# A fused windowed attention and squared-ReLU MLP on one NeuronCore: the written-out order of all engines, banks, buffers and first loads is replaced by another one

## The chip, the core and the metric

The kernel runs on one NeuronCore of a Trainium2 chip. The core has TensorE (PE in the profile, with its weight loads as PEld), VectorE (DVE), ScalarE (ACT), GpSimd (POOL) and SyncE (SP), 16 DMA engines, an on-chip memory of 128 partitions and a small accumulator memory of eight banks. The metric is the device time of one execution in microseconds (us). The profiled execution is described by its span, from the first to the last instruction.

## What is computed

The input is q, k and v of 4 batches, 8 heads, 768 positions and 64 channels. Each position attends to itself and the 95 positions before it, and to the first 8 positions of its batch; a slope per head lowers the scores with distance. The heads are put side by side (3072 tokens of 512 numbers) and go through an MLP with a hidden width of 2048.

```python
scores = scale * np.matmul(q, k.transpose(0, 1, 3, 2))
bias = -slopes[:, None, None] * dist[None, :, :]
scores = np.where(keep, scores + bias[None], -1000000000.0)
a = softmax(scores)                       # over the last axis
x = np.matmul(a, v)                       # heads side by side: [3072, 512]
h = x @ w_in                              # [3072, 2048]
r = np.maximum(h, 0.0)
out = (r * r) @ w_out                     # [3072, 512]
```

## The kernel before

**Attention.** The 3072 tokens are 24 tiles of 128 (tile j, six per batch). For a tile, q and k are brought into transposed form (qkT). For tiles 0 to 7 TensorE does that (words `tr.0.j` for q and `tr.1.j` for k, line 528) and VectorE or ScalarE copies the result out of its bank (`T.n.j`, lines 455 and 453). For tiles 8 to 23 one DMA transpose on SP's queue does it (`T.j`, line 554). Then follow the bias products of tiles 0 to 2 (`bias.j`, line 597), the scores against the tile itself and the one before it (`sc.j`, line 618; those of tiles 7, 13 and 19 ride along with the tile before), four exponentials on ScalarE (`exp.j`, line 684; two for the first tile of a batch), the multiplication with the decay on VectorE (`mul.j`, line 709), the products with v (`pv.j.0`, `pv.j.1`, line 767) and the normalisation on VectorE (`norm.j`, lines 797 and 798). `gk.j` and `gv.j` copy the eight global keys and values of a batch into the tile's own buffers. The finished tile x is transposed again, by TensorE (`trx.j`, line 835, and a copy `xT.j`) for tiles 0 to 7 and by a DMA transpose on SP's queue (`xT.j`, line 859) from tile 8 on.

**MLP.** Two tiles make a block of 256 tokens, 12 blocks. Both layers use a scheme with seven products in the place of eight: sums of operand quarters are made first (`isum` and `wsum` of the weights, `xs` of the inputs, line 939, and `sum` of the hidden values, line 1185, all on VectorE), then seven products (`h.blk.g.p1` to `p7`, line 967, eight matmuls each; `s2.blk.p.g`, line 1230, four matmuls each), which are taken apart again by copies (`u` and `part`, mostly ScalarE), additions (`c`, line 1011, and `o`, line 1305, VectorE), rectifiers (`relu` and `c21`) and squares (`q`, `sq`, mostly ScalarE). Block 0 and half of block 1 use plain products (`s1.blk.s`, line 1081), which need only a slice s of the first weights.

**Loads.** The q and k of tile 0 come over SP's queue (line 343). All else of the first part comes over POOL's queue, one transfer after the other, by line 330 (`ld.q.j`, `ld.k.j`, `ld.v.j`, then `ld.win.s` and `ld.wout.s`, the slices of the two weights; slices 0 and 2 of the first come in two halves). From tile 6 on `load.j` issues v, q and k of a tile (line 334). q and k have three buffers for the tiles from 6 on, so `load.j` waits until tile j-3 has been transposed; v has ten. `gate.j` is a small write of VectorE that stands for a buffer of v being free. Results leave by SP's queue (`st.blk.sub`, line 1327).

**What sets the order.** Nothing is scheduled on the chip. A string of 1230 words, `ORDER`, lists every operation once. The program walks through it and emits each operation to its engine. A word's tail gives the bank (`:3`) or buffer that it takes, and `@A` or `@V` the engine, ScalarE or VectorE, where there is a choice. So the string sets the sequence on each engine's own queue, the banks and buffers, and the engine. The place of a word among words of other engines has no effect. Engines run ahead of each other until a data dependence or a buffer still in use holds them; within an engine the order is strict, so an instruction that waits holds all that stand behind it.

```python
for word in ORDER.split():
    word, _, banks = word.partition(":")
    name, _, letter = word.partition("@")
    o["engine"] = self.ENGINES[letter] if letter else next(iter(o["engines"]))
    o["banks"] = [int(b, 16) for b in banks]
```

Of the kernel before, what the change touches and what calls it, by code (L numbers as in the profile page):

```python
# [57 lines left out]
tr.0.0:0 T.0.0@V tr.1.0:1 bias.0.0:23 T.1.0@V ld.q.1 ld.k.1 tr.0.1:4 T.0.1@V ld.q.2 ld.k.2 E0.1 ld.q.3 ld.v.0 ld.k.3  # L58
tr.1.1:5 T.1.1@A ld.v.1 sc.0.0 bias.1.0:6701 exp.0.1.0:0 sc.1.0 tr.0.2:4 exp.0.0.0 gk.1@A T.0.2@V exp.1.0.0:1 tr.1.2:5
T.1.2@V bias.2.0:3264 sc.2.0 exp.1.1.0 exp.1.1.1:3 ld.k.4 exp.1.0.1 ld.q.4 pv.0.1:5 tr.0.3:7 pv.0.0:1 ld.v.2 gk.2@A  # L60
exp.2.1.1:4 exp.2.0.0:5 exp.2.0.1 exp.2.1.0 tr.1.3:0 T.0.3@V T.1.3@V sc.3.0:4730 norm.0.0:0 norm.0.1 pv.1.0:6 tr.1.4:1
ld.q.5 pv.1.1:2 norm.1.0:1 norm.1.1 trx.0:5 exp.3.1.1:6 ld.k.5 gv.1@A ld.v.3 tr.0.4:0 T.1.4@V T.0.4@V xT.0@A:0 gk.3@V
trx.1:6 exp.3.0.1 exp.3.1.0:7 exp.3.0.0 ld.win.1.0 pv.2.0:2 pv.2.1:5 norm.2.0:0 norm.2.1 gv.2@V mul.3.0:8 sc.4.0:1037
exp.4.1.0:9 trx.2:2 ld.win.4.0 xT.1@A exp.4.1.1:a tr.1.5:4 tr.0.5:5 T.1.5@A exp.4.0.0 xT.2@A:1 mul.3.1:b pv.3.0:0
pv.3.1:6 T.0.5@A s1.0.1:7 norm.3.0:1 gk.4@V exp.4.0.1 norm.3.1 gv.3@A s1.0.1#2 trx.3:4 sc.5.0:0126 exp.5.0.1:c
exp.5.1.0:d s1.0.4:5 exp.5.1.1 E0.0 mul.4.0:e xT.3@V ld.v.4 mul.4.1:f ones.6 pv.4.0:3 s1.1.1:4 relu.0.4@V:2 exp.5.0.0
ld.win.3.0 s1.0.3:2 pv.4.1:1 relu.0.1@A:0 sq.0.1@A:0 gv.4@A s1.0.3#2 mul.5.1:1 s1.1.3:6 norm.4.0:0 norm.4.1 ld.win.2.0
ld.win.0.0 s1.0.0:5 relu.0.3@A:3 sq.0.3@A mul.5.0:5 gate.10 s1.0.2:0 trx.4:7 relu.1.1@A:4 sq.1.1@A:1 xs.1.0:0 ld.v.5
ld.win.2.1 pv.5.0:3 ld.win.0.1 pv.5.1:1 xs.1.1 ld.win.6.0 ld.win.7.0 ld.win.5.0 relu.1.3@A:7 norm.5.0:1 norm.5.1
ld.wout.3 s1.1.2:2 xT.4@A:2 relu.1.2@A:8 ld.wout.2 ld.wout.1 ld.wout.0 isum.0.0 s1.1.0:4 s1.0.2#2 trx.5:3 gate.14  # L70
# [1379 lines left out]
```

## Time and profile before

| what | before |
|---|---|
| runs | 197.19, 198.71 and 276.52 us; the median is 198.71 us |
| span of the profiled execution | 195.7 us; its own run time is not listed, the two lower runs lie 1.5 and 3.0 us above this span |
| matmuls on TensorE | 2808 |
| moved by DMA | 26.92 MB in 111713 packets |
| VectorE, ScalarE, POOL busy | 179.4, 161.6 and 75.1 us |

The third run is far above the other two; the comparison below goes by the lower ones and by the span. The profile has one row for a group of instructions of one engine and line, with its number, busy time and mean duration, and behind a bar the time that the engine idled ahead of them and what ended it. In a timeline row the first number is the start in us from the beginning of the span, the second the length of the row. In the windows view the columns are the stretch, its length, the busy time and instruction count of PE, PEld, DVE, ACT and POOL, the granted clock of TensorE as a share of its full speed, the DMA load and GB/s. Matmuls overlap one another and their ends are modelled, so a busy TensorE need not be one at its peak rate.

### The profile page before, as it was taken

To read this page: it belongs to the slowest core of one execution; us is meant where nothing else is said; L and a number is where in the kernel's file an instruction comes from. 1 tells how busy PE (TensorE), PEld (TensorE's weight loads), DVE (VectorE), ACT (ScalarE), POOL (GpSimd) and SP (SyncE) were. 2 spreads that over 40 slices of the span, in tenths; PEclk is the share of its full clock that TensorE was granted. 3 is DMA by queue.
4 is the path that set the end of the run, shared out by engine and by line. 5 is a ranking of instruction groups with operands and counts; after the bars stand their busy time and mean duration, and the time that the engine had idled before them with its cause. 6 is when DMAs were issued, how large, how long until landed. Compare 5 with 4: busy or idle time off the path is not lost.

```text
span 195.7 us, 6835 instructions
## 1 busy us (share of the span) xinstructions
PE 188.5 (96%) x2808; PEld 170.5 (87%) x2808; DVE 179.4 (92%) x437; ACT 161.6 (83%) x338; POOL 75.1 (38%) x93
## 2 busy tenths in 40 slices
PE   7986999999999999999999999999999999999993
PEld 3774999999888989989989989989889999999982
DVE  8569989999999999989999999899999899999982
ACT  6699999999989797999899997587987798986600
POOL 8999784775564502650047080119200000000000
PEclk9999999999999999999999999999999999999999
DMA  7999999999999999999949989999947440152026
GB/s 125 149 150 167 179 193 205 205 162 151 155 150 143 99 177 168 119 100 227 139 79 129 138 74 119 209 168 97 147 113 188 85 136 13 20 193 105 0 91 234
DMA packets 111713, 26.92 MB, mean 138 GB/s; under 512 B 103234, under 2 KB 108866, under 8 KB 111682
## 3 DMA queue, kind: packets, MB, share of 16 engines
q0 software_dynamic: 80256, 13.37, 91.9%
q1 hardware_dynamic: 31426, 13.11, 33.4%
q8 instruction: 22, 0.36, 0.7%
q14 instruction: 9, 0.07, 0.1%
HBM read 27.26 MB, written 6.29 MB: 171 GB/s over the span
## 4 chain that ended last, share of the span: by engine, by line
PE 85%; POOL 6%; DMA 5%; DVE 1%; issue 0%; POOLq 0%; DVEq 0%
PE bank L1230 37%; PE bank L967 32%; PE bank L1081 6%; PE bank L618 5%; PE bank L767 5%; POOL qk_first L330 5%; DMA win<-in_moe_w_in_dram 3%; DMA xT<-x 2%; POOL v L330 2%; PE bank L835 1%; PE bank L528 0%; DVE xs L939 0%; DVE buf L886 0%; DVE hsum L1185 0%; DVE early L1305 0%
## 5 line engine op out<-in xcount | busy, mean ns | idle before, releaser
L684 ACT ACTIVATE buf<-bank 128x512 bf16<-128x512 f32 x76 | 41.5, 613 | 2.8 <-PE bank L618 2.7
L1031 ACT ACTIVATE hs<-buf 128x512 bf16<-128x512 f32 x62 | 37.2, 635 | 2.5 <-DVE buf L1011 2.0
L1230 PEld LDWEIGHTS <-hsum 128*128 128x128 bf16 x384 | 35.3, 98 | 4.0
L453 ACT COPY buf<-bank 128x512 f32<-128x512 f32 (+1 forms) x59 | 32.1, 569 | 7.7 <-PE bank L967 6.1
L1230 PE MATMUL bank<-wsum,hsum 128*128 128x256 bf16 x288 | 38.0, 273 | 0.0
L1011 DVE CUSTOM_DVE_ANT_0 buf<-bank,buf 128x512 f32<-128x512 f32 x49 | 33.0, 682 | 0.8 <-ACT buf L453 0.3
L967 PEld LDWEIGHTS <-qk_first 128*128 128x128 bf16 x504 | 31.1, 98 | 1.4 <-issue 0.3
L967 PEld LDWEIGHTS <-win 128*128 128x128 bf16 x504 | 30.8, 98 | 0.9
L334 POOL DMA_DIRECT2D qk<-in_q_dram x18 | 16.0, 889 | 35.3 <-DMA qkT<-qk 30.0
L1230 PEld LDWEIGHTS <-hs 128*128 128x128 bf16 x288 | 26.3, 98 | 2.7
L1230 PE MATMUL bank<-wout,hs 128*128 128x256 bf16 x192 | 27.3, 273 | 0.0
L334 POOL DMA_DIRECT2D v<-in_v_dram x18 | 16.0, 891 | 23.1 <-PE bank L967 13.1
L967 PE MATMUL bank<-xs,qk_first 128*128 128x128 bf16 x336 | 24.6, 219 | 0.2 <-DVE buf L886 0.2
L967 PE MATMUL bank<-xT,win 128*128 128x128 bf16 x336 | 24.6, 219 | 0.0
L709 DVE TENSOR_TENSOR buf<-buf,E 128x1024 bf16<-128x1024 bf16 x32 | 21.5, 683 | 0.5 <-ACT buf L684 0.5
L798 DVE TENSOR_TENSOR x<-bank,rs 128x256 bf16<-128x256 f32 x48 | 20.4, 425 | 1.7
L767 PE MATMUL bank<-v,buf 128*128 128x65 bf16 x312 | 16.1, 193 | 0.9 <-DMA v<-in_v_dram 0.5
L1185 DVE TENSOR_TENSOR hsum<-hs 128x1024 bf16<-128x1024 bf16 (+1 forms) x26 | 16.4, 642 | 0.3
L334 POOL DMA_DIRECT2D qk<-in_k_dram x18 | 16.1, 897 | 0.6 <-DMA wout<-in_moe_w_out_dram 0.4
L767 PEld LDWEIGHTS <-buf 128*128 128x128 bf16 x312 | 13.9, 98 | 1.8 <-DVE buf L709 0.6
L884 ACT ACTIVATE buf<-bank 128x512 f32<-128x512 f32 x23 | 13.7, 607 | 1.0 <-PE bank L967 1.0
L453 ACT COPY part<-bank 128x256 f32<-128x256 f32 x29 | 11.1, 383 | 3.6 <-PE bank L1230 3.6
(92 smaller groups left out, 349.4 us busy)
## 6 DMA issues: line engine op xcount, KB each, us to landing
out_dram<-buf SPq DMA_DIRECT2D x17, 256.0 KB, 2.7
v<-in_v_dram POOLq DMA_DIRECT2D x24, 128.0 KB, 5.4
qk<-in_q_dram POOLq DMA_DIRECT2D x18, 128.0 KB, 5.0
qk<-in_k_dram POOLq DMA_DIRECT2D x18, 128.0 KB, 5.5
wout<-in_moe_w_out_dram POOLq DMA_DIRECT2D x8, 256.0 KB, 9.7
win<-in_moe_w_in_dram POOLq DMA_DIRECT2D x6, 256.0 KB, 7.1
out_dram<-early SPq DMA_DIRECT2D x5, 256.0 KB, 2.7
qk_first<-in_q_dram POOLq DMA_DIRECT2D x5, 128.0 KB, 4.6
```

Of the source, the lines that this page charges most:

```text
L334: nc.gpsimd.dma_start(out=dst, in_=src)
L453: nc.scalar.copy(dst, src)
L684: nc.scalar.activation(out=tiles[tag, j, g][:, odd], in_=tiles.pop(("sc", j, odd, g)).rearrange("p a c -> p (a c)"), func=Act.Exp, scale=s ...
L709: nc.vector.tensor_mul(at, tiles.pop(("esc", j, g)), bias)
L767: nc.tensor.matmul(out=po[:, hi, :], lhsT=tiles["at", j, g][:, odd, at * P : (at + 1) * P], rhs=v_sb[kj][:, h, :], start=(i == 0), stop=(i ...
L798: nc.vector.tensor_tensor(out=x[:, 4 * hf : 4 * hf + 4, :], in0=po[:, :, :D], in1=rs.to_broadcast([P, 4, D]), op=Alu.mult,)
L884: nc.scalar.activation(dst, src, Act.Relu)
L967: nc.tensor.matmul(out=tiles["h", blk, g, bank][:, n], lhsT=left_[:, s, k], rhs=right_[:, k], start=opens and n == 0 and k == 0, stop=k == ...
L1011: nc.vector._custom_dve(TENSOR_ADD_SAT, out=hr, in0=src, in1=tiles.pop(("u", blk, g, i)), s0=float("inf"), s1=0.0,)
L1031: nc.scalar.activation(hs, hr, Act.Square)
L1185: nc.vector.tensor_tensor(out=t[:, i, h], in0=t[:, a, h] if isinstance(a, int) else half_a(blk, *a)[:, h], in1=t[:, b, h] if isinstance(b, ...
L1230: nc.tensor.matmul(out=tiles["acc", blk, bank][:, cols], lhsT=left_[:, s], rhs=right_[:, cols], start=first and s == 0, stop=s == NSTEP - ...
```

## The change

Only the string `ORDER` is replaced; not a line of code differs. The 1230 names are the same, so every load, matmul, copy and store is still made once. What differs is the sequence on each engine, the bank and buffer numbers, the order of the first loads and, for some words, the engine. Of the words with a choice of engine VectorE has 11 fewer than before among `c21`, `gv`, `part`, `u`, `sq` and `o.p4`, and 7 more among `T`, `gk`, `xT` and `q`; ScalarE has the balance of four more. The diff holds 111 lines on each side; the first of each side, and the lines that hold the words `T.11` and `xT.9`, read:

```diff
-tr.0.0:0 T.0.0@V tr.1.0:1 bias.0.0:23 T.1.0@V ld.q.1 ld.k.1 tr.0.1:4 T.0.1@V ld.q.2 ld.k.2 E0.1 ld.q.3 ld.v.0 ld.k.3
+ld.k.1 ld.q.1 ld.q.2 ld.k.2 tr.0.0:0 ld.v.0 tr.1.0:1 T.0.0@V ld.k.3 bias.0.0:23 T.1.0@V tr.1.1:0 bias.1.0:4567 ld.v.1
...
-h.3.1.p4 c.3.1.c21@A:1 q.3.1.c11@A c.3.1.c12:6 s2.2.p5.0 pv.9.0:5 gk.9@V T.11 st.0.0 norm.9.0:1 q.3.1.c12@A
-xT.9 norm.10.0:0 xs.4.0:1 xs.4.1 h.4.1.p2:5 pv.10.1:4 q.3.1.c21@A q.3.0.c21@A part.3.p6@A:1 u.4.1.1@A:6 u.4.0.1@A:5
+o.2.p5:9 xT.9 q.3.0.c12@V h.3.0.p4 exp.10.1.0:b s2.3.p1.0:6 exp.10.1.1:e sum.3.2:1 s2.3.p1.1 T.11 o.2.p4@A sum.3.0
```

POOL's queue, ahead of and at the first slices of the first weights (`win`). The names are the load targets; in both versions the rows further up are the other loads of q and k (of tiles 1 to 5, `qk_first`) and v. Before:

```order
L330 DMA qk_first_66<-in_q_dram 128x8x64
L330 DMA v_2_73<-in_v_dram 128x8x64
L330 DMA qk_first_66<-in_q_dram 128x8x64
L330 DMA qk_first_66<-in_k_dram 128x8x64
L330 DMA v_3_74<-in_v_dram 128x8x64
L330 DMA win_93<-in_moe_w_in_dram 128x4x256 x2
L330 DMA v_4_75<-in_v_dram 128x8x64
```

Now:

```order
L330 DMA v_2_73<-in_v_dram 128x8x64
L330 DMA qk_first_66<-in_q_dram 128x8x64
L330 DMA qk_first_66<-in_k_dram 128x8x64
L330 DMA qk_first_66<-in_q_dram 128x8x64
L330 DMA v_3_74<-in_v_dram 128x8x64
L330 DMA win_93<-in_moe_w_in_dram 128x4x256 x2
L330 DMA v_4_75<-in_v_dram 128x8x64
```

In both, five loads of q, five of k and four of v stand ahead of the first `win`. What moved is which of them come first: k of tile 1 now leads, the last q stands one load later and the last k one load earlier, and v of tile 5, just below these rows, now stands behind three slices of the weight instead of behind five pieces of it.

TensorE's queue around the first plain product of the MLP (L1081), with the weight loads. `win_93` is the first weight, `v_3` and `buf_8` belong to the second half of tile 3's product with v, `qkT_5` and `qkT_4` to the scores of tile 5. Before:

```order
L767 LDWEIGHTS buf_8_135
L767 MATMUL bank_6_113<-v_3_74,buf_8_135 128x65
L767 LDWEIGHTS buf_8_135
L767 MATMUL bank_6_113<-v_2_73,buf_8_135 128x65
L1081 LDWEIGHTS win_93
L1081 MATMUL bank_7_114<-xT_0_117,win_93 128x128
```

Now:

```order
L618 LDWEIGHTS qkT_4_85
L618 MATMUL bank_7_114<-qkT_5_86,qkT_4_85 128x128
L618 LDWEIGHTS qkT_4_85
L618 MATMUL bank_4_111<-qkT_5_86,qkT_4_85 128x128
L1081 LDWEIGHTS win_93
L1081 MATMUL bank_1_108<-xT_0_117,win_93 128x128
```

The scores of tile 5, which stood after the first product of the MLP and the transposes of tile 3, now stand directly ahead of it.

SP's queue around block 8. `xT_1` (before) and `xT_0` (now) is the transposed input of block 8 (tiles 16 and 17, from `x_0` and `x_1`), `qkT_8`, `qkT_7` and `qkT_6` are q and k of tiles 20, 19 and 18. Before:

```order
L859 DMA_TRANSPOSE xT_1_118<-x_0_115 128x4x128
L1327 DMA out_0_dram<-buf_11_138 128x512
L554 DMA_TRANSPOSE qkT_8_89<-qk_8_69 128x8x128
L859 DMA_TRANSPOSE xT_1_118<-x_1_116 128x4x128
L1327 DMA out_0_dram<-early_103 128x512
L554 DMA_TRANSPOSE qkT_7_88<-qk_7_68 128x8x128
L1327 DMA out_0_dram<-buf_9_136 128x512
L554 DMA_TRANSPOSE qkT_6_87<-qk_6_67 128x8x128
```

Now:

```order
L859 DMA_TRANSPOSE xT_0_117<-x_0_115 128x4x128
L859 DMA_TRANSPOSE xT_0_117<-x_1_116 128x4x128
L554 DMA_TRANSPOSE qkT_8_89<-qk_8_69 128x8x128
L554 DMA_TRANSPOSE qkT_7_88<-qk_7_68 128x8x128
L554 DMA_TRANSPOSE qkT_6_87<-qk_6_67 128x8x128
L554 DMA_TRANSPOSE qkT_9_90<-qk_6_67 128x8x128
```

The second transpose of block 8's input (tile 17) stood behind a store and the transpose of tile 20; now it stands ahead of tile 20, and no store stands between them. The same kind of exchange is made the other way round further up: the transpose of tile 11 (`T.11`) stood ahead of `xT.9` and now stands behind it, and that of tile 15 now stands behind `xT.12`, where it stood ahead of it.

More of the change, by code (lines that the diff above doesn't have):

```diff
@@ L63 @@
[L63 to L67, printed above, removed]
```

212 lines of the change are left out of this document (109 added, 103 removed).

## The prediction

> **What bounds the kernel now.** I read the totals of the page first, then the windows, then the chain of work that ended last, then the waits of TensorE.
>
> ```profile
> span 195.7 us, 6835 instructions
> PE 188.5 (96%) x2808; PEld 170.5 (87%) x2808; DVE 179.4 (92%) x437; ACT 161.6 (83%) x338; POOL 75.1 (38%) x93
> ```
>
> TensorE is busy for 96% of the span, VectorE for 92%. An average does not say where the missing 7.2 us of TensorE are, so I cut the span at 4.58 us (end of the warm-up matmuls), 19.66 us (first plain product of the MLP) and 192.40 us (end of the last matmul).
>
> ```profile
> 4.58:19.66 15.08, 12.57 (x213) 10.04 (x212) 11.19 (x34) 13.03 (x31) 15.08 (x19) 1.00 2.17 155
> 19.66:192.40 172.74, 172.55 (x2588) 159.23 (x2588) 164.11 (x384) 145.82 (x304) 56.22 (x67) 1.00 1.21 136
> ```
>
> The reader is to see two stages with different limits. In the first, TensorE idles 15.08 - 12.57 = 2.5 us. In the second it idles 0.2 us in 172.7, at a granted clock of 1.00. POOL, which issues the loads, is busy all through the first stage.
>
> ```profile
> 13.60 6.01 DMA win<-in_moe_w_in_dram
> 19.66 1.07 PE bank L1081 x16
> ...
> 35.40 3.13 PE bank L967 x56
> ...
> 123.03 4.44 DMA xT<-x
> 128.31 0.60 DVE hsum L1185
> 128.91 0.61 DVE buf L886
> ...
> 182.77 9.64 PE bank L1230 x88
> ```
>
> The chain says the same. Up to 19.66 us it runs through POOL's issues and the landing of the first weight slice, then through TensorE nearly without a break: a product of 128 columns takes 3.13/56 = 0.056 us and one of 256 columns 9.64/88 = 0.110 us, back to back. One detour is left, at 123 to 129.5 us: the second transpose of block 8's input lands 4.44 us after its issue.
>
> A new order does not shorten a matmul. In the second stage it can win the 0.2 us of shown idle time and what the modelled ends of matmuls hide, some tenths; in the first at most the 2.5 us. After the last matmul both strings have the same words up to the last store. So the most that the change can bring is about 2.7 us of 195.7, or 1.4%, below the 2% that a measurement of this kernel can tell from no change. What it can lose has no such bound.
>
> **The first stage.** The first weight slice is what ends it.
>
> ```profile
> PE bank L1081 <- DMA win<-in_moe_w_in_dram: 0.3, 1, 0.3
> 13.60 1.62 POOL L330 DMA_DIRECT2D win<-in_moe_w_in_dram  x2
> DMA to landing us min/median/max: 6.6/6.6/6.6
> ```
>
> TensorE waited 0.3 us for it. POOL issues it behind 14 loads in the old order and behind 14 in the new one, each of the same size, so it lands at 13.60 + 6.01 = 19.6 us again. The second slice is issued right behind it (the third row is its landing; 14.34 + 6.6 = 20.96 us).
>
> ```profile
> 16.35 0.23 PE L618 MATMUL bank<-qkT 64*128 64x128 bf16 x2
> 20.88 0.23 PE L618 MATMUL bank<-qkT 64*128 64x128 bf16 x2
> 21.44 1.05 PE L1081 MATMUL bank<-xT,win 128*128 128x256 bf16 x8
> ```
>
> These are the starts of tile 4's scores, of tile 5's scores and of the second slice's product. Ahead of that product the same work stands in both orders: all of tiles 0 to 3, the scores of tiles 4 and 5, the first slice's product, the transposes of tiles 0 to 3. So its start compares the two stages. Before, it is 21.44 us.
>
> In the new order tile 4's scores stand behind the transpose of k of tile 5, which is now the 12th load of POOL; the 12th of before was issued at 11.00 us.
>
> ```profile
> 11.00 0.98 POOL L330 DMA_DIRECT2D qk_first<-in_q_dram  x1
> DMA to landing us min/median/max: 5.6/5.6/5.6
> ```
>
> It lands at 16.6 us, and with the transpose and the copy (the row below shows such a copy, 0.6 us on ScalarE) tile 4's scores start near 16.9 us instead of 16.35. Its exponentials are then later by the same half microsecond. Against that, tile 5's scores no longer wait for ScalarE.
>
> ```profile
> 17.58 0.61 PE L528 MATMUL bank<-ident,qk_first 128*128 128x128 bf16 x8
> 18.23 0.60 ACT L453 COPY qkT<-bank 128x512 bf16<-128x512 bf16 x1
> 19.66 0.65 ACT L453 COPY qkT<-bank 128x512 bf16<-128x512 bf16 x1
> L684 ACT ACTIVATE buf<-bank 128x512 bf16<-128x512 f32 x76 | 41.5, 613 | 2.8 <-PE bank L618 2.7
> ```
>
> Before, both transposes of tile 5 were done at 18.2 us, but the second copy ended only at 20.3 us, behind other work of ScalarE. Now both copies are on VectorE. The scores of tile 5 then wait for two exponentials of tile 4 whose banks they take, 41.5/76 = 0.55 us each (last row), which start at 18.5 us behind two copies and a global one of ScalarE, and end near 20.0 us; the first slice's product follows (20.0 to 20.9), the transposes of tile 3 (to 21.1), and the second slice has landed. Its product starts at 21.1 us: **0.3 us gained**. Bounds: it cannot start ahead of the landing at 20.96, so at most 0.45 gained; if the exponentials of tile 4 stay late by the half microsecond to the end, 0.5 lost. I take 0.3, which is what the rows give when followed one by one; the cover is VectorE, which in this stage is busy 11.2 of 15.1 us.
>
> What stands behind (slices 3, 2, 0, then 6, 7, 5 and all of `wout`) lands in the same slots as before. The new order uses several of them within 0.2 us of their landing, so a gain beyond 0.3 us would be taken back there.
>
> **The detour at 123 us.** VectorE waited for the transpose of tile 17's x:
>
> ```profile
> 127.55 0.42 DVE L939 TENSOR_TENSOR xs<-xT 128x512 bf16<-128x512 bf16 x1 [0.52 <-DMA xT<-x]
> 120.48 2.07 SPq L554 DMA_TRANSPOSE qkT<-qk  x1
> 123.03 1.19 SPq L859 DMA_TRANSPOSE xT<-x  x1
> DMA to landing us min/median/max: 2.4/2.7/5.5
> ```
>
> The last row is over all 16 transposes of x. This one took 4.4 us with the transpose of tile 20 ahead of it in flight; the median is 2.7. Now tile 20 comes behind it. It lands 1.7 us sooner; the first consumer of it (`xs.8.0`) stands three products of 0.445 us earlier in TensorE's order, 1.3 us. So the 0.5 us wait goes, and TensorE, which waits for VectorE right behind it (the two DVE pieces of the chain), has most of it: **0.4 us gained**. Bounds: 0.5 gained, or nothing if it is as slow as before. What is late next is VectorE itself, which has no room there.
>
> **Engines exchanged.** VectorE gives four words net to ScalarE, one of 0.3 to 0.7 us each, some 2 us of 179.4. TensorE waits for VectorE only 0.2 us in the second stage, so this is worth 0 to 0.2 us; I take 0. ScalarE, at 83%, covers it.
>
> **Transposes that come later in SP's queue.** This is what the change may cost. T.11 now stands behind xT.9, T.15 behind xT.12, and the scores of tile 17 stand 2.0 us earlier in TensorE's order while T.17 is held by the same load.
>
> ```profile
> 71.39 1.20 SPq L859 DMA_TRANSPOSE xT<-x  x1
> 78.13 0.23 PE L618 MATMUL bank<-qkT 64*128 64x128 bf16 x2
> 96.20 3.03 SPq L859 DMA_TRANSPOSE xT<-x  x2
> 101.04 0.23 PE L618 MATMUL bank<-qkT 64*128 64x128 bf16 x2
> 107.33 1.23 SPq L554 DMA_TRANSPOSE qkT<-qk  x1
> 115.06 0.23 PE L618 MATMUL bank<-qkT 64*128 64x128 bf16 x2
> DMA to landing us min/median/max: 3.1/5.2/6.7
> ```
>
> The last row is over the transposes of q and k; the L618 rows are the scores of tiles 11, 15 and 17. T.11 is issued behind xT.9 at 71.4 + 1.3 = 72.7 us and lands between 75.8 and 79.4 us, 77.9 at the median; the scores are wanted at 78.1 - 0.3 = 77.8 us. xT.12 was issued at 96.2 us, right behind its normalisation; that now stands about 1.8 us earlier, so T.15 goes at 94.4 + 1.2 = 95.6 us and lands between 98.7 and 102.3, against 100.7 us wanted. T.17 goes at 107.3 us and lands between 110.4 and 114.0, 112.5 at the median; it is wanted at 115.06 - 2.0 - 0.3 = 112.8 us. At the medians these waits cost 0.1 to 0.2 us together; at the maxima 1.6 + 1.6 + 1.2 = 4.4 us; at the minima nothing. Behind a waiting score matmul stands all of TensorE's queue. I take **0.2 us lost** and keep both ends.
>
> **The sum.** 195.7 - 0.3 - 0.4 + 0.2 = 195.2 us of span. The two lower runs of before lie 1.5 and 3.0 us above the span of the profiled one; the listed median, 198.7, is the upper of them. With the middle, 2.3, the changed kernel comes to **197.5 us**.
>
> **Rivals.** *Nothing gained:* VectorE is busy 164.1 of 172.7 us, so what TensorE gains in front is waited for behind VectorE, and T.11 eats the rest. Span 195.5 to 196.5, time about 198.2 us. For it: VectorE stands at 95% in the second stage. Against it: it loses 2 us of work.
>
> *Late transposes (slower):* the transposes of q and k meet other traffic and take 6.7 us, not 5.2. The row above has 3.1 to 6.7 us for the same transfer, so it can happen. Then 4.4 us are lost at tiles 11, 15 and 17, and if those of x take 5.5 us in the place of 2.7, the inputs of blocks 6 and 8 are late by some 1.4 us each: 195.7 - 0.3 + 4.4 + 2.8 = 202.6 of span, up to 205 us of time, and some 200 us with half of it. It decides where the landings rise above 5.1 to 5.5 us, the leads of these three tiles. There is a second turn of the screw: a tile's buffer of q and k is filled anew only when its transpose has landed.
>
> ```profile
> POOL qk L334 <- DMA qkT<-qk: 30.0, 6, 9.9
> ```
>
> POOL waited 30 us for that, in six waits, so each late transpose delays a later load as well. Against this rival: T.12 and T.13 have 10 us of TensorE work between their place and their scores, counted from the new order. The Trainium skill, DMA: Bandwidth & Descriptors, section SWDGE vs HWDGE vs iDMA, says that POOL's and SP's transfers feed different queues inside each DMA engine and that the engine takes them in turn. By that rule a transpose that meets a load takes twice the quiet time; the trace agrees, with 3.1 us at the least and 6.7 at the most, but cannot say which of the new places meet one; if all did, the time would be that of this rival.
>
> *All idle time of the front goes:* tiles 0 to 5 pass without a wait and the 2.5 us are won, 192.7 of span, 195 us. Against it stands the first slice at 19.6 us, whose place in POOL's queue is the same. This is also the case in which the change would not do what it seems: the loads are put in another order, but the one that ends the stage stays where it was.
>
> **How the numbers follow.** The forecast (span 194.6 to 195.5) has 0.53, nothing gained 0.26, late transposes 0.18, the front emptied 0.03. The range reaches down to 194.6 + 1.5 = 196.1, and a little below it for half of the last case, 195.6; up to 202.4, which takes in the lower half of the late transposes. Slower by over 2% is above 202.7 us: 0.13. Faster by over 2% is below 194.7 us: 0.03. The rest, 0.84, is within 2%.
>
> **What would show it.** Right: the second slice's product (L1081, 128x256) starts at 21.0 to 21.2 us; the `xs` row near 127 us has no wait for `xT`; TensorE's waits show none above 0.3 us for `qkT` after 20 us. Wrong: a wait of L618 for DMA `qkT<-qk` near 78, 101 or 113 us, a wait of more than 1 us for `win` or `wout` between 20 and 45 us, or a stage after 20 us in which TensorE's busy time falls below 9.8 of 10 us without a DMA named, which would put VectorE's order in the place of the transposes.

## The result and the profile after

The changed kernel takes 198.94 us at the median of 14 runs (198.02 to 200.55), the kernel before 197.51 us at the median of 14. The ratio is 1.0072 with a 95% interval of 1.0047 to 1.0097: slower by 0.7%, which is less than 2% and more than the measurement is uncertain. The ratios, here and below, leave out the slow runs (here one of 276.52 us), and so can differ a little from the ratio of the medians. 197.5 us and a gain of 0.5 us of span had been forecast. The profiled execution of the changed kernel took 198.99 us, so it is a typical one.

First the totals of the page of the changed kernel, then the same two stretches as before (stretch, length, busy time and count of PE, PEld, DVE, ACT and POOL, granted clock, DMA load, GB/s).

```profile
span 197.2 us, 6882 instructions
PE 187.9 (95%) x2808; PEld 170.0 (86%) x2808; DVE 176.9 (90%) x433; ACT 165.8 (84%) x342; POOL 75.1 (38%) x93
```

```profile
4.58:19.66 15.08, 11.68 (x217) 9.63 (x217) 12.70 (x41) 12.56 (x28) 15.08 (x19) 1.00 2.19 158
19.66:193.90 174.24, 172.88 (x2588) 158.91 (x2584) 160.15 (x372) 150.49 (x310) 56.23 (x67) 1.00 1.20 136
```

The span is 1.5 us longer, the same 2808 matmuls run at the same clock of 1.00, and VectorE has 2.5 us less to do. TensorE now idles 3.4 us in the first stretch, where it idled 2.5, and 1.4 us in the second, where it idled 0.2. So the loss is waiting. How it falls on the two stages this cut does not tell, because the first plain product of the MLP now starts at 20.33 us and not at 19.66; the sums further down do. Who was waited for, in waits of TensorE (total us, times, longest), before:

```profile
PE bank L618 <- DVE qkT L455: 0.6, 1, 0.6
...
PE bank L767 <- DMA v<-in_v_dram: 0.5, 1, 0.5
...
PE bank L967 <- DVE buf L886: 0.2, 1, 0.2
```

Now, and in the chain of work that ended last (start, length):

```profile
PE bank L618 <- DVE qkT L455: 1.3, 2, 0.7
PE bank L767 <- DMA v<-in_v_dram: 1.3, 2, 0.9
...
PE bank L967 <- DMA win<-in_moe_w_in_dram: 0.6, 1, 0.6
...
PE bank L967 <- DMA xT<-x: 0.3, 1, 0.3
```

```profile
24.02 8.90 DMA win<-in_moe_w_in_dram
32.99 1.43 DVE qk_first L907 x3
117.87 6.86 DMA xT<-x
```

The first two rows of waits belong to the first stage; the L618 row is longer because tile 4's scores now wait for VectorE's copies. The third row is new: slice 5 of the first weights, the last to be loaded, lands at 24.02 + 8.90 = 32.9 us and first TensorE, then VectorE's sums of the weights wait for it. The same load in the kernel before:

```profile
L330 POOL DMA_DIRECT2D win<-in_moe_w_in_dram x1: 740/740/740, 23.4 to 23.4; - x1
DMA to landing us min/median/max: 7.6/7.6/7.6
```

It landed at 31.0 us, 1.9 us earlier. The last row of the chain is the transposed x of tile 16, which takes 6.9 us. The two places at which the prediction looked:

```profile
21.60 0.28 PE L1081 MATMUL bank<-xT,win 128*128 128x256 bf16 x1
```

```profile
128.07 0.42 DVE L939 TENSOR_TENSOR xs<-xT 128x512 bf16<-128x512 bf16 x1
```

The second slice's product starts at 21.60 us, not at 21.0 to 21.2. VectorE's wait for the transposed x of tile 17 is gone, as forecast (no bracket behind the row), but nothing was won by it.

One trace is one execution. To add up where TensorE loses time I took, for every matmul of a trace, the time from the start of the one before to its own, less the time that such a matmul takes when they run back to back (0.0556 us for 128 columns, 0.109 for 256, and so on), and summed the rest. The first column of sums ends at the second slice's product, ahead of which the same work stands in both orders; some 0.12 us at each change to score matmuls are in all of them. The traces marked 2 and 3 are from the experiments below.

```
us lost by TensorE    start of    up to  from there          53 to  108 to  after
beyond its own rate   2nd slice   it     to 53 us   108 us   130 us  130 us  sum
before                21.44       4.67   0.40       2.17     0.62    1.24    9.11
before, 2             21.30       4.54   0.40       1.84     0.61    1.24    8.64
changed               21.60       4.81   1.53       2.07     0.89    1.27    10.56
changed, 2            20.96       4.13   1.33       1.99     1.34    1.37    10.16
changed, 3            20.81       4.17   0.27       2.21     1.12    1.30    9.07
mean of changed less
mean of before        -0.25       -0.24  +0.64      +0.08    +0.50   +0.07   +1.05
```

On the mean of these traces the first stage wins its quarter of a microsecond. Behind it 0.6 us are lost up to 53 us and 0.5 us between 108 and 130 us. The traces differ by a microsecond among themselves, so the means are rough, and more traces change the first two of them.

Some experiments below alter nothing ahead of 53 us. With them there are six traces of the new order and four of the old for that part (two more of the old are left out, in which the granted clock was 0.66 between 19 and 24 us).

- The second slice's product starts at 20.6 to 22.5 us in the new order and at 21.3 to 21.4 us in the old, at 21.3 us on the mean in both. In the new order it follows the landing of its slice by 0.05 to 0.27 us, in the old by 0.5 to 0.95 us.
- From there to 53 us the loss is 0.2 to 1.5 us in the new order and 0.4 to 0.8 us in the old, some 0.3 us more on the mean.

So neither the gain in front nor the size of the loss up to 53 us is settled. The 0.5 us between 108 and 130 us holds: three more traces of the old order, unaltered there, lose 0.3 to 0.6 us.

### The profile page after: what moved, and what is told of

Its sections match the earlier page's. It is cut to its first block, busy times and chain, and to the rows that moved or that the text cites. A ratio compares the mean times of both kernels' runs of the same rounds, so it can differ in the third digit from the quotient of the medians.

```text
span 197.2 us, 6882 instructions
## 1 busy us (share of the span) xinstructions
PE 187.9 (95%) x2808; PEld 170.0 (86%) x2808; DVE 176.9 (90%) x433; ACT 165.8 (84%) x342; POOL 75.1 (38%) x93
## 4 chain that ended last, share of the span: by engine, by line
PE 76%; DMA 12%; POOL 8%; DVE 2%; issue 1%; DVEq 0%; POOLq 0%
PE bank L1230 36%; PE bank L967 30%; DMA win<-in_moe_w_in_dram 8%; PE bank L618 5%; POOL qk_first L330 5%; PE bank L767 4%; DMA xT<-x 3%; POOL v L330 2%; POOL win L330 1%; DVE qk_first L907 1%; PE bank L528 0%; PE bank L1081 0%; DVE x L798 0%; DVE buf L1305 0%; DVE buf L1011 0%
## 5 line engine op out<-in xcount | busy, mean ns | idle before, releaser
L1031 ACT ACTIVATE hs<-buf 128x512 bf16<-128x512 f32 x54 | 33.1, 638 | 0.9 <-DVE buf L1011 0.5
L453 ACT COPY buf<-bank 128x512 f32<-128x512 f32 (+1 forms) x51 | 28.2, 569 | 6.2 <-PE bank L967 5.2
L684 ACT ACTIVATE buf<-bank 128x512 bf16<-128x512 f32 x54 | 30.3, 615 | 2.0 <-DVE buf L709 1.4
L967 PEld LDWEIGHTS <-qk_first 128*128 128x128 bf16 x504 | 30.5, 98 | 0.7
L334 POOL DMA_DIRECT2D qk<-in_q_dram x18 | 16.0, 888 | 33.8 <-DMA qkT<-qk 30.8
L1230 PE MATMUL bank<-wout,hs 128*128 128x256 bf16 x192 | 25.9, 273 | 0.0
L334 POOL DMA_DIRECT2D v<-in_v_dram x18 | 16.1, 895 | 21.3 <-PE bank L967 12.0
L1011 DVE CUSTOM_DVE_ANT_0 buf<-bank,buf 128x512 f32<-128x512 f32 x32 | 21.4, 684 | 0.4 <-ACT hs L1031 0.2
L684 ACT ACTIVATE early<-bank 128x512 bf16<-128x512 f32 x34 | 19.2, 607 | 1.5 <-PE bank L618 0.9
L884 ACT ACTIVATE buf<-bank 128x512 f32<-128x512 f32 x26 | 15.3, 599 | 3.2 <-PE bank L967 2.0
L453 ACT COPY part<-bank 128x256 f32<-128x256 f32 x32 | 12.2, 382 | 4.1 <-PE bank L1230 4.1
L1305 DVE TENSOR_TENSOR buf<-bank,part 128x256 f32<-128x256 f32 x30 | 12.5, 419 | 1.7 <-PE bank L1230 1.1
L767 PE MATMUL bank<-v,buf 128*128 128x65 bf16 x256 | 12.7, 194 | 1.3 <-DMA v<-in_v_dram 1.3
```

The costliest lines, as they stand in the source:

```text
L334: nc.gpsimd.dma_start(out=dst, in_=src)
L453: nc.scalar.copy(dst, src)
L684: nc.scalar.activation(out=tiles[tag, j, g][:, odd], in_=tiles.pop(("sc", j, odd, g)).rearrange("p a c -> p (a c)"), func=Act.Exp, scale=s ...
L767: nc.tensor.matmul(out=po[:, hi, :], lhsT=tiles["at", j, g][:, odd, at * P : (at + 1) * P], rhs=v_sb[kj][:, h, :], start=(i == 0), stop=(i ...
L884: nc.scalar.activation(dst, src, Act.Relu)
L967: nc.tensor.matmul(out=tiles["h", blk, g, bank][:, n], lhsT=left_[:, s, k], rhs=right_[:, k], start=opens and n == 0 and k == 0, stop=k == ...
```

## The experiments

The theories, as the expectations name them. **L**: the new order of the first loads makes them land late. **C**: the new order of the compute engines loses, whatever the loads do. **F**: an instruction fetch holds up one of the 16 DMA engines. **L2**: TensorE cannot pass the first use of slice 5, so that a late landing there is paid in full. **T**: the transposes near 113 and 123 us come too late.

### Once more, both kernels

The changed kernel, unaltered:

> The changed kernel once more, unaltered, with a fresh trace. In the first trace weight slice 5 (the last of the first weight) landed at 32.9 us, 1.9 us later than before the change, and TensorE fell 1.5 us back between 20 and 53 us. If the late landings belong to the new string, slice 5 lands at 32.5 to 33.3 us again and the span is 196.9 to 197.6 us. If they are the luck of one execution (one of the 16 DMA engines held up by an instruction fetch), slice 5 lands anywhere from 31.0 to 33.0 us and the span follows it, 195.5 to 197.5 us, while the median time stays 0.7% above that of before.

The kernel before, unaltered:

> The kernel before once more, unaltered, for a second trace. If its landings belong to its string, slice 5 lands at 30.8 to 31.3 us again, span 195.4 to 196.0 us. If the landings are luck, slice 5 can come at up to 33 us here too, with a span of about 196.5 to 197.

Measured: the changed kernel 198.60 us at the median of 10 runs, ratio 1.0031 (0.9991 to 1.0072), span 196.8 us. The kernel before 197.17 us, span 195.4 us. In the new trace of the changed kernel, the chain of work that ended last and one of TensorE's waits:

```profile
23.36 8.45 DMA win<-in_moe_w_in_dram
...
101.91 6.52 DMA qk<-in_k_dram
108.48 5.50 DMA qkT<-qk
117.54 6.68 DMA xT<-x
```

```profile
PE bank L618 <- DMA qkT<-qk: 0.7, 1, 0.7
```

Slice 5 lands at 31.8 us, 1.1 us sooner than in the first trace, so its lateness varies from one execution to the next. In its place the scores of tile 17 wait 0.7 us for their transpose, which waits for the load of k of tile 17. That is the wait which the prediction's second rival had named. The landings are partly luck, and the time stays up nevertheless.

### Each half alone

The new order of the engines with the old order of the first loads (nothing else of the queues differs):

```diff
-ld.k.1 ld.q.1 ld.q.2 ld.k.2 ld.v.0 ld.k.3 ld.v.1 ld.q.3 ld.k.4 ld.v.2 ld.q.4 ld.k.5 ld.q.5 ld.v.3
-ld.win.1.0 ld.win.4.0 ld.v.4 ld.win.3.0 ld.v.5 ld.win.2.0 ld.win.2.1 ld.win.0.1 ld.win.0.0
+ld.q.1 ld.k.1 ld.q.2 ld.k.2 ld.q.3 ld.v.0 ld.k.3 ld.v.1 ld.k.4 ld.q.4 ld.v.2 ld.q.5 ld.k.5 ld.v.3
+ld.win.1.0 ld.win.4.0 ld.v.4 ld.win.3.0 ld.win.2.0 ld.win.0.0 ld.v.5 ld.win.2.1 ld.win.0.1
 ld.win.6.0 ld.win.7.0 ld.win.5.0
```

> The new order of all engines with the old order of the first loads. Theory L (the new order of loads is what lands late): slice 5 lands near 31.0 us as before, the 1.5 us come back, time 0.992 to 1.000 of before (the 0.3 us of the first stage may show). Theory C (the new order of the compute engines is what loses, whatever the loads do): time 1.004 to 1.010 of before. Theory F (instruction fetches hold up one DMA engine, at places that depend on the program): slice 5 anywhere from 31 to 33 us, and the time goes with it.

The old order of the engines with the new order of the first loads (the same lines the other way round; the string has a line less, so its line numbers are one lower):

> The old order of all engines with the new order of the first loads. Theory L: slice 5 lands at 32.5 to 33.3 us, TensorE falls back between 20 and 45 us, time 1.004 to 1.012 of before. Theory C: landings may differ, the time is 0.998 to 1.003 of before. Theory F: slice 5 from 31 to 33 us, and the time goes with it.

Measured: 198.84 us, ratio 1.0067 (1.0027 to 1.0106), and 198.56 us, ratio 1.0043 (1.0015 to 1.0070). Slice 5 landed at 30.8 and 30.5 us. Both halves are slower. The old order with the new loads loses in the first stage, by TensorE's waits:

```profile
PE bank L527 <- DMA qk_first<-in_q_dram: 1.1, 2, 0.7
```

An order of the engines and an order of the loads go together there; this kernel says nothing on what the full change loses. The other one has the old loads and the whole loss of the changed kernel, with slice 5 on time: L falls, and something besides slice 5 must cost as much. The number is the one that C expects. Its trace was its quickest execution (197.56 us), so I took a second one:

> A second trace of the new order with the old loads, whose first trace was its fastest run (197.6 us against a median of 198.8). Theory L2 and T: near 199 us one sees a wait for slice 5 near 32 us, or for the transpose of tile 17 near 113 us, or for the transposed x near 123 us, 0.8 to 1.5 us together more than in the first trace. Theory C: waits of TensorE for VectorE or ScalarE instead.

Measured: 199.22 us, span 197.4 us. The first of its waits of TensorE:

```profile
PE bank L967 <- DMA xT<-x: 1.5, 1, 1.5
```

The transposed x of tile 16 was issued at 117.0 us and took 8.1 us. In the sums above this trace has 1.98 us between 108 and 130 us, and its quicker twin 0.92. The five traces of the new order with its later loads and transposes as they are have 0.89 us or more in this stretch, the two of the kernel before 0.62 and 0.61. So in this stretch it is the new order that loses, as C says, but not by VectorE or banks: what TensorE waits for is a DMA, as T says.

### The price of a late slice 5

The kernel before, with one slice of the second weights ahead of slice 5:

```diff
-ld.win.7.0 ld.win.5.0 ld.wout.3 ld.wout.2
+ld.win.7.0 ld.wout.3 ld.win.5.0 ld.wout.2
```

> The kernel before, with one edit: the first slice of the second weight (wout 3, 256 KB, one slot of 1.3 us) goes ahead of slice 5 of the first weight, so that slice 5 lands 1.3 us later, near 32.2 us, and nothing else in front of it moves. Prices the landing. Theory L2 (TensorE cannot pass the third matmul of block 2's product h.2.1.p1, which needs slice 5): in the old order that matmul stands near 32.0 us, 1.0 us behind the landing of 31.0; the delay costs 0.2 to 0.5 us at TensorE and up to 0.4 more behind VectorE's sums of the weights: time 1.001 to 1.006 of before. Theory that landings there have slack: 0.999 to 1.001.

Measured: 198.06 us, ratio 1.0030 (0.9995 to 1.0065). Slice 5 landed at 32.0 us, 1.0 and 1.4 us later than in the two traces of the kernel before, and between the second slice's product and 53 us TensorE lost 1.04 us where it lost 0.40. So a microsecond or so of lateness costs some 0.6 us in the old order too: L2 holds, within what was expected.

Then both orders with a lighter first weight, so that everything behind it should land a microsecond sooner:

```diff
     def load_w_in(s):
         n = 2 if s in TWO else 1
+        if s == 6:
+            swdge(("win", 6, 0), w_in_sb[6][:, :1], moe_w_in[:P, 12 * P : 14 * P]...)
+            return
...
+    nc.vector.memset(w_in_sb[6][:, 1:], 0.0)
```

> The kernel before with a lighter first weight: of slice 6 only the first quarter is loaded, the rest of it is set to zero by one VectorE write early on (the output is not the reference's). Every landing behind it comes about 1.0 us earlier, slice 5 near 30.0 us. Theory L2: the old order has 1.0 us of slack there already, so almost nothing is won: 0.998 to 1.001 of before (the extra write of VectorE can cost 0.2 us).

> The changed kernel with the same lighter slice 6. Theory L2 (what the new order loses is the late landing of slice 5): slice 5 lands 1.0 us earlier and the waits of 0.3 to 1.1 us near 32 and 35 us go; ratio to before 0.999 to 1.002, against 1.003 to 1.007 of the unaltered one. Theory T (it loses at the late transposes near 113 and 124 us): stays at 1.003 to 1.007. Theory C (VectorE's new order): the same, with waits of TensorE for VectorE.

Measured: 197.59 us, ratio 0.9991 (0.9941 to 1.0041) for the old order, 198.34 us, ratio 1.0027 (0.9978 to 1.0075) for the new one. Slice 5 landed at 30.2 and 30.4 us and no wait for it is left in either trace. The old order won nothing, as expected. The new one has 1.0027, against 1.0031 to 1.0075 in the three series of the changed kernel. By the ratio that is up to half of the loss, by the medians (198.34 against 197.35 us, 0.5%) hardly any, and the intervals overlap. So this run does not show what late weights cost; it shows that they are not the whole. Its trace, of its quickest execution (197.02 us), has only 0.30 us between 108 and 130 us, so the late transposes are not in every execution either.

### The transpose of tile 17

POOL's queue in the changed kernel ahead of that transpose (start, length, and in brackets what ended POOL's idle time):

```profile
101.24 0.88 POOL L334 DMA_DIRECT2D v<-in_v_dram  x1 [12.03 <-PE bank L967]
102.10 0.89 POOL L334 DMA_DIRECT2D qk<-in_q_dram  x1
102.97 0.90 POOL L334 DMA_DIRECT2D qk<-in_k_dram  x1
```

These are v, q and k of tile 17. POOL has been idle for 12 us because v's buffer was not free; q and k, whose buffer was free, stand behind it. First q and k ahead of v in every tile:

```diff
             def emit_load(e, j=j):
-                load_v(j)
                 load_part(0, j)
                 load_part(1, j)
+                load_v(j)
```

> The changed kernel with one edit: from tile 6 on, a load word issues q, k and then v, in the place of v, q, k. So k of tile 17 is issued one slot (0.87 us) earlier, and its transpose, which waits for it, goes 0.9 us earlier. Theory T: the wait of the scores of tile 17 (0.9 us in the second trace, 0 in the first) and part of the wait for the transposed x near 124 us (0.3 to 0.6 us) go, ratio to before 0.998 to 1.004. Theory L2: no change in the time, 1.003 to 1.007, with waits near 32 and 35 us as before.

Measured: 198.85 us, ratio 1.0064 (1.0025 to 1.0102). The wait of tile 17's scores is gone, and TensorE loses 0.7 us near 91 us in its place. It waits there for a multiplication of VectorE, which stands behind a sum of inputs (`xs`) that has waited for the transposed x of tile 11:

```profile
90.48 0.43 DVE L939 TENSOR_TENSOR xs<-xT 128x512 bf16<-128x512 bf16 x1 [0.90 <-DMA xT<-x]
```

That transpose took 6.3 us here, 5.4 to 5.7 us in the three traces of the changed kernel (where VectorE waits at most 0.3 us for it) and 3.8 and 3.9 us in the two of the kernel before.

So then for tile 17 alone (`if j == 17:` q, k, v; the others as they were; the line numbers are three higher):

> The changed kernel; q and k go ahead of v in the load of tile 17 alone, so that the transpose of tile 17, which waits for k, goes 0.9 us earlier and no other tile's v is late. Theory T (the late transposes carry much of the loss): no wait of the scores of tile 17 near 113 us, ratio to before 0.999 to 1.004, 0.2 to 0.4% below the unaltered one. Theory L2: waits for slice 5 near 32 us stay, ratio 1.003 to 1.007.

Measured: 197.47 us, ratio 1.0017 (0.9981 to 1.0053). POOL and SP in that kernel:

```profile
93.10 0.88 POOL L334 DMA_DIRECT2D qk<-in_q_dram  x1 [6.17 <-DMA qkT<-qk]
93.96 0.89 POOL L334 DMA_DIRECT2D qk<-in_k_dram  x1
98.89 1.75 POOL L334 DMA_DIRECT2D v<-in_v_dram  x2 [4.03 <-PE bank L970]
```

```profile
L557 SPq DMA_TRANSPOSE qkT<-qk x1: 2203/2203/2203, 100.3 to 100.3; - x1
DMA to landing us min/median/max: 9.3/9.3/9.3
```

k went 9 us earlier, not the 0.9 that I had expected, since only v had been held. The transpose went at 100.3 in the place of 106.5 to 109.1 us; it took 9.3 us and still landed at 109.6, well ahead of the scores at 112 us. Seven of the ten runs lie at 197.72 us or below; of the 34 runs of the unaltered changed kernel three do.

Both reliefs together:

> The changed kernel with both reliefs: of slice 6 of the first weight only a quarter is loaded (the output is not the reference's) and q and k go ahead of v for tile 17. If the two kinds of late landings are all that the new order loses, it is now level with the kernel before or its light version: ratio to before 0.995 to 1.001, TensorE's stalls after 20 us as small as before (3.9 to 4.6 us in all). If the new order loses elsewhere (VectorE, banks), the ratio stays at 1.003 or more.

Measured: 197.59 us, ratio 1.0023 (0.9990 to 1.0055). The two gains do not add up. With slice 5 and tile 17 out of the way the trace loses 0.82 us between 90 and 100 us and 0.93 between 100 and 110 us, where the kernel before loses 0.24 and 0.45, in pieces of 0.2 to 0.3 us. The new order has more places where a landing is just in time than the two that I had picked.

A third series of the unaltered changed kernel, on the same chip as three runs further down (tile 18 in either kernel, and the transposed x of tile 17 ahead of the transpose of tile 20 alone):

> The changed kernel unaltered, a third trace and a third set of times, so that the next kernel can be compared with it on the same chip. Ratio to before 1.003 to 1.008. Theory T expects its stalls mostly near 113 us (transpose of tile 17) and 122 us (transposed x of tile 16), theory L2 near 32 us (slice 5).

Measured: 198.81 us, ratio 1.0075 (1.0041 to 1.0109). The trace is of its quickest execution (197.45 us): slice 5 landed at 30.6 us and cost nothing, and 0.84 us were lost ahead of the matmul at 123.2 us.

```profile
123.24 1.07 PE L967 MATMUL bank<-xT,win 128*128 128x128 bf16 x16 [0.68 <-DVE hsum L1185]
```

```profile
L859 SPq DMA_TRANSPOSE xT<-x x1: 1193/1193/1193, 116.0 to 116.0; - x1
DMA to landing us min/median/max: 7.2/7.2/7.2
```

The first row puts the wait down to VectorE; the second view shows that the transposed x of tile 16 landed at 116.0 + 7.2 = 123.2 us, just ahead of the matmul that reads it.

### The detour at 123 us, which was to be won

The prediction had put it down to the transpose of tile 20 ahead of it. One piece of the change alone, in the kernel before, with TensorE's and VectorE's queues untouched:

```diff
-xT.16:1 st.4.0 T.20 xT.17 st.3.0
+xT.16:1 xT.17 st.4.0 T.20 st.3.0
```

> The kernel before with one piece of the change alone: on SP's queue the transposed x of tile 17 goes ahead of a store and of the transpose of tile 20; TensorE's and VectorE's sequences stay. My forecast for this piece was 0.4 us: the wait of VectorE for xT near 127 us (0.5 us) goes. If so, ratio 0.997 to 0.999. If the transpose of tile 17 is as slow there, or the transpose of tile 20 is late in its place, 0.999 to 1.003.

Measured: 198.21 us, ratio 1.0035 (1.0003 to 1.0066). The trace is of its longest execution, so only the place is read from it, on VectorE:

```profile
129.33 0.69 DVE L1011 CUSTOM_DVE_ANT_0 buf<-bank,buf 128x512 f32<-128x512 f32 x1 [1.39 <-DMA out_dram<-buf]
```

The store that had been passed now leaves late, and VectorE waits 1.4 us for the buffer that it empties. So the transposed x ahead of the transpose alone, behind the store:

```diff
-xT.16:1 st.4.0 T.20 xT.17 st.3.0
+xT.16:1 st.4.0 xT.17 T.20 st.3.0
```

> The kernel before; on SP's queue the transposed x of tile 17 goes ahead of the transpose of tile 20 but stays behind the store of block 4, whose late landing cost the earlier form 1.2 us. If the transpose of tile 20 made it slow: it lands 1 us sooner, the wait of 0.5 us goes, ratio 0.997 to 0.9995. If the load of v does: no gain, and the transpose of tile 20, now 3 us later, delays the loads behind it: 0.999 to 1.003.

Measured: 197.31 us, ratio 1.0004 (0.9977 to 1.0030). The transposed x:

```profile
L859 SPq DMA_TRANSPOSE xT<-x x1: 1197/1197/1197, 122.9 to 122.9; - x1
DMA to landing us min/median/max: 4.2/4.2/4.2
```

It goes at the same time as before (x of tile 17 is not ready sooner) and takes 4.2 us in the place of 4.4. The transpose of tile 20 was not the cause. What else is in flight is on POOL's queue, in the trace of the kernel before:

```profile
122.60 0.88 POOL L334 DMA_DIRECT2D v<-in_v_dram  x1 [4.76 <-issue]
```

A load of v, issued 0.4 us ahead. Two runs were meant to move it:

> The kernel before with q and k ahead of v in the load of tile 18. That v was issued at 122.6 us, 0.4 us ahead of the transposed x of tile 17 (landed 127.27 and 127.46 us). If the transfer in flight is what made that transpose slow, it lands in 2.4 to 3.5 us in the place of 4.4, VectorE's wait of 0.5 us near 127 us goes, and 0.2 to 0.4 us are won: ratio 0.997 to 0.9995. If the transpose of tile 20 ahead of it was the cause, as I had forecast, nothing changes: 0.999 to 1.002.

> The changed kernel with q and k ahead of v in the loads of tiles 17 and 18. Tile 17 as in the run before this series (0.4% won there); with tile 18, whose v was the last transfer issued ahead of the transposed x of tile 16 (it landed at 124.9, the transposed x at 124.7 us), that transposed x lands about 0.7 us sooner and TensorE's wait for it near 122 us (0.3 to 1.7 us) shrinks by as much. Theory T: ratio to before 0.996 to 1.001. If the transposed x does not follow the loads ahead of it: 1.000 to 1.004.

Measured: 197.38 us, ratio 1.0007 (0.9979 to 1.0035), and 198.18 us, ratio 1.0019 (0.9990 to 1.0048). Neither tests what its expectation says. I had taken the v at 122.6 us (118.1 us in the new order) for that of tile 18; by the order of the load words, 19, 20, 18 and then 22 or 23, it is the first transfer of the word behind. The second of them still carries the edit of tile 17. Beside the third series of the changed kernel, on the same chip, it points the way of that edit: 198.18 against 198.81 us, ratio 1.0019 against 1.0075, with intervals that overlap. Its trace, of an execution of 199.73 us, waits 0.7 us for another transposed x near 101 us.

With the right words:

> The kernel before with q and k ahead of v in the load of tile 22, whose v is the transfer issued at 122.6 us, 0.4 us ahead of the transposed x of tile 17. If the load in flight makes that transpose slow, it now takes 2.4 to 3.5 us, VectorE's wait of 0.5 us near 127 us goes and 0.2 to 0.4 us are won: ratio 0.997 to 0.9995, and this is the quickest version. If stores and the transpose of tile 20 make it slow, it still takes 4.2 to 4.5 us: 0.999 to 1.002.

> The changed kernel with q and k ahead of v in the loads of tiles 17 and 23. The v of tile 23 (not of 18, as the run before this took it) is the transfer issued 0.3 us away from the transposed x of tile 16 in all traces of the new order; with the edit it goes behind q and k of tile 23, which are held up to some 10 us longer. If the transposed x lands when the loads issued ahead of it have landed, it lands 0.8 to 1.5 us sooner, near the landing of k of tile 18, and the wait near 122 us (0.3 to 1.7 us) goes: ratio to before 0.996 to 1.001, and 0.003 to 0.007 below the changed kernel. If not: 1.000 to 1.004, as with tile 17 alone.

Measured in the kernel before: 197.08 us, ratio 0.9992 (0.9978 to 1.0006), with the quickest median of all kernels here, though it cannot be told from the kernel before. The transposed x of tile 17 and VectorE's first use of it (line numbers three higher):

```profile
L862 SPq DMA_TRANSPOSE xT<-x x1: 1197/1197/1197, 122.6 to 122.6; - x1
DMA to landing us min/median/max: 2.4/2.4/2.4
```

```profile
126.51 0.41 DVE L942 TENSOR_TENSOR xs<-xT 128x512 bf16<-128x512 bf16 x1
```

2.4 us in the place of 4.4, with the transpose of tile 20 still ahead of it, and no wait of VectorE. So the load of v in flight made it slow. The other traces agree: in all eight of the old order with that load in its place, the transposed x lands 0.2 us behind the landing of that load (at 127.46 and 127.27 us in the first). TensorE lost 0.28 us between 108 and 130 us, against 0.61 and 0.62.

Measured in the changed kernel: 197.93 us, ratio 1.0042 (1.0017 to 1.0068). The transposed x of tile 16:

```profile
L862 SPq DMA_TRANSPOSE xT<-x x1: 1192/1192/1192, 117.9 to 117.9; - x1
DMA to landing us min/median/max: 4.6/4.6/4.6
```

It lands 2.2 us sooner than the 6.9 us of the changed kernel, and TensorE's loss in the stretch falls from 0.89 to 0.38 us. The loads ahead of it were issued earlier here as well, so that this run does not tell the two apart; why it still takes 4.6 us, with no load issued in the 5 us ahead of it, stays open. Nor was the v of tile 23 issued 0.3 us from it in all traces, as the expectation has it: 0.3 and 1.3 us behind it in the first two and 0.7 us ahead in the third. The time does not follow. In this trace TensorE loses 0.8 us at 92 us, again behind VectorE's wait for the transposed x of tile 11, which took 6.4 us. It was issued at 84.5 us, ahead of the altered loads, so the edit did not make it late.

```profile
91.01 0.42 DVE L942 TENSOR_TENSOR xs<-xT 128x512 bf16<-128x512 bf16 x1 [0.98 <-DMA xT<-x]
```

## Why the prediction was wrong

Two steps failed. Around 123 us a gain was forecast, 0.2 us net of the late transposes, and 0.5 us were lost. And the landings that are used with next to no slack were priced at nothing, where 0.3 to 0.6 us were lost. The first of the two is the better shown.

**That the gain is bounded by what TensorE idles, and the loss is not:** right, and it should have weighed more. Behind the first stage TensorE had 0.2 us of shown idle time to give, and by the sums above it lost some 1.3 us there (some 1.0 us with the further traces).

**The first stage, 0.3 us gained:** right in kind, not shown in size. The second slice's product starts at 21.60, 20.96 and 20.81 us in the three traces of the changed kernel, 21.1 on the mean, against 21.44 and 21.30; over the six and four traces named above the gain is nothing. What was right is the bound: the product now follows the landing of its slice at once, where it was 0.5 to 0.95 us behind it. So an early landing is won here and a late one is paid. One can't forecast a tenth here, since the first slice itself landed between 18.6 and 20.3 us in the 20 traces.

**"What stands behind ... lands in the same slots as before. The new order uses several of them within 0.2 us of their landing, so a gain beyond 0.3 us would be taken back there": this step failed.** It gave the uses next to no slack and set no price on that. A landing is not a time but a spread: slice 5, behind the same loads in both strings, landed between 30.4 and 32.9 us in the traces, in the old order (30.5 to 32.7) as in the new (30.4 to 32.9). A use without slack pays every lateness. The run in which slice 5 was made late gives the price, some 0.6 us for 1.0 to 1.4 us. In the sums this term is +0.64 us, some 0.3 us with the further traces, and I had 0 for it. How much of it is the new order and how much the luck of the executions is not settled, by the light first weight neither.

**The detour, 0.4 us gained:** failed, in the step that named the transpose of tile 20 as what made the transposed x slow. It was the load of v, 2.4 against 4.4 us. In the changed kernel the transposed x of tile 17 does land 2.4 us after its issue and its wait is gone, as forecast. But the x of tile 16 stands ahead of it, with six loads of 0.9 us each issued between 113.8 and 118.1 us, and takes 6.9, 6.7 and 7.2 us in the three traces. The wait moved one transposed tile ahead and grew: TensorE loses 0.3 to 1.7 us at it in the five traces of the new order, and 0.35 us behind VectorE's wait in the two of the kernel before. The first and last of these loads in the trace of the changed kernel (the start, the length and what ended POOL's idle time):

```profile
113.82 0.88 POOL L334 DMA_DIRECT2D qk<-in_q_dram  x1 [6.45 <-DMA qkT<-qk]
...
118.14 0.93 POOL L334 DMA_DIRECT2D v<-in_v_dram  x1
```

**Late transposes, 0.2 us lost, at most 4.4:** right in kind, at tile 17 as named. The changed kernel pays 0 to 0.9 us there, because its scores stand 2 us earlier and its load does not: k is held behind v. No wait was seen for T.11 or T.15. With the detour this makes +0.50 us between 108 and 130 us where -0.2 were forecast. That tile 17 matters is supported, not shown, by the edit that loads its q and k first. The ratio is 1.0017 alone, 1.0019 with tile 18 and 1.0042 with tile 23, against 1.0031 to 1.0075, with intervals that overlap. Of the 34 runs of these three kernels 14 lie at 197.72 us or below, of the 34 unaltered ones three.

**Engines exchanged, 0:** not contradicted. VectorE lost 2.5 us of work, and the time did not gain by it. In the first stage TensorE waits longer for VectorE's copies (the L618 rows, 1.3 us for 0.6); no run changes the engines alone.

**From span to time, 2.3 us:** too much. Every run on record that lists both lies 1.7 to 1.9 us above its span, so the forecast span of 195.2 us stands for 197.0 us of time. Two sums of the rivals are off as well: with the 2.5 us of the first stage won the span is 193.2 us, not 192.7, and half of the late transposes makes 201 us, not 200.

**The rivals.** The truth is a weak form of the second, slower one, with the weights beside the transposes. I gave it 0.18 and looked for it at 200 to 205 us, as if all its waits fell into one execution. The traces of the new order have one to three of them each, and its series are 0.3 to 0.75% slower. "Nothing gained" put the time at 198.2 us, nearer to the truth than the forecast, for a reason that did not hold: in the places above TensorE waited for a DMA, not for VectorE's own work. The Trainium skill, DMA: Bandwidth & Descriptors, section SWDGE vs HWDGE vs iDMA, says that the queues are taken in turn inside a DMA engine. One load ahead does nearly double the time of a transpose here (2.4 to 4.4 us), in agreement with it; a row of loads makes it 6.4 to 8.1 us, which is more than twice.

What is not settled: that the loss is waiting for late transfers is what the traces show, but the shares of the places are not, and neither is it shown that relieving them brings the time back. The edits that come nearest to the kernel before (1.0017 to 1.0023) can't be told from it, and hardly from the unaltered new order. With two places relieved (slice 5 and tile 17) the ratio was still 1.0023, and in three other altered kernels a further place came up, the transposed x of tile 11 near 91 us. No version here is quicker than the kernel before by more than the measurement can tell.

## What to carry to other kernels

When an order is moved closer to its landings, price each landing by its spread over several traces, not by its place in one: a use with no slack pays all lateness. Look in each queue for a transfer that is ready but stands behind one that is not (k of tile 17 behind v), and for loads in flight ahead of a transpose that TensorE waits for. One trace of a kernel whose runs differ by a microsecond can show the right place and the wrong cause; take two or three before naming one.

## What was not expected of the hardware

The same load at the same place of the same queue landed up to 2.5 us apart (slice 5, 30.4 to 32.9 us), at a granted clock of 1.00. Part of the lateness came in single steps of 0.9 to 1.4 us at one transfer, where the queue's usual distance is 1.3 us; the transfer behind followed in 0.6 to 1.1 us. Slice 5 took such a step in three traces with its load in place, the first two of the changed kernel and one of the old order (the transposed x of tile 17 ahead of the transpose of tile 20 alone). Each time an instruction fetch of 16 KB started between the landing of the slice ahead and its own (at 30.6 us in the first). But twelve other traces have such a fetch at the same place and no step there, so theory F is not borne out, and what makes the steps stays open.

A DMA transpose of one x tile took 2.4 us with no load issued close ahead of it. It took 4.2 to 4.6 us with one load of 128 KB issued 0.3 to 0.5 us ahead, and landed 0.2 us behind that load in all eight traces. Beside a row of loads, the last of them issued within 1.5 us of it, it took 6.4 to 8.1 us; it landed within 0.3 us of one of the last two loads in five traces, and 1.3 to 2.0 us behind the last in three, which stays open. The transpose of tile 17, issued into such a row, took 9.3 us.
